# VectorE's order in eight recurrence units: masks, states, subtractions, then the next unit's products and scans

## The chip, the cores and the metric

The kernel runs on one core of one Trainium2 chip. The metric is device time in microseconds (us), the median of several runs. Five engines work side by side and each runs its own instructions strictly in the order in which they were written out: TensorE (PE, matrix products), VectorE (DVE), ScalarE (ACT), GpSimd (POOL), and SyncE (SP), which here only issues DMA transfers. They wait for one another through semaphores.

## The reference

The inputs pass through three layers. The first is a recurrence over 768 tokens (2 sequences, 8 heads of width 48) with a state of 48 by 48 per head; the second a gated two-layer product (weights `w_k`, `w_r`, `w_v`); the third a gated layer with mixing over tokens (`w_in`, `w_sg`, `w_out`).

```python
for t in range(S):                                   # layer 1
    cur = einsum('bhd,bhe->bhde', u * k_t, v_t)
    y[:, :, t] = einsum('bhd,bhde->bhe', r_t, state + cur)
    state = w_t[..., None] * state + einsum('bhd,bhe->bhde', k_t, v_t)
# layer 2, x_prev = x shifted by one token
xk = mu_k * x + (1 - mu_k) * x_prev
xr = mu_r * x + (1 - mu_r) * x_prev
x = sigmoid(xr @ w_r) * (relu(xk @ w_k) ** 2 @ w_v)
# layer 3
u, v = split(gelu(x @ w_in));  v = layernorm(v) * g
out = x + (u * (w_sg @ v + b_sg)) @ w_out
```

## The kernel before

**Units of the recurrence.** The tokens are cut into four groups of 384, and the eight heads into four pairs. A unit is one pair of heads in one group; the code numbers units from 0 to 15, four to a group, and so does this text (the units 9 to 16 of the change's description, counted from one, are the code's 8 to 15). A unit treats its 384 tokens as three chunks of 128 and replaces the loop over t by scans and matrix products:

- *Scans* on VectorE (`scans`, L444 to L449): running products of the decay, forward (`pf`) and backward (`pr`), with a small reciprocal between them.
- *Products* (`products`, L453 and L456): `kp` = k times `pr`, `rp` = r times `pf`.
- Step S on TensorE (`attn_sc`): it transposes `kp` (`kt_ps`, L476), forms the bonus `ab` from two halves of r times k times u (`rh`; the high half by ScalarE at L521, the low one by VectorE at L523; L495 and L496 read them), and multiplies `kp` with `rp` (`sc`, L500).
- *Masks* on VectorE (L532): `am`, the causal part of `sc`. Just ahead of them VectorE multiplies `ab` with v (L503, tile `ru`). GpSimd's only piece of a unit is the product `ru` of the next unit (L466); it may start when L503 is done, and the halves `rh` of the next unit follow it.
- Step K (`attn_kv`): state increments `kv` (L552). *States* on VectorE (L562 and L564): `zt`, the state after each chunk; ScalarE scales them into `sblk` and `scar` (L578), four and two small copies per unit.
- Step Y (`attn_y`): v times `am` (L596). Step Z (`attn_z`): the scaled states times `rp` are added (L610). VectorE then adds the bonus (`yo`, L620), and SyncE copies `yo` to its place in `xx` (L631).

**The projections beside them.** Layer 2 of group s runs on TensorE between the steps of the four units of group s+1. In the stretch of this study these are products of 128 by 128 by 384 in pieces: every weight and every activation is held as a high and a low half (a value rounded to a shorter format and what is left), and each product is three matrix products. The pieces: eight blocks `k`, three blocks `r`, three blocks `v`. After each `k` block ScalarE does three operations (`kr` relu, L735; `kh` square into the high half, L756; `kr` square in place, L757), and VectorE the *subtraction* `kl` = square minus high half (L758). Two buffers hold `kr`, so the relu of block f waits for the subtraction of block f-2. The low halves of the weights (`wkl`, `wrl`, `wvl`, one subtraction each at L332) are made once, in the units 8 to 11: 8 + 3 + 8 of them.

**What sets the order.** TensorE's instructions are written by hand in the order of `plan`. For the other engines the code gives each instruction a due time (`at`), and a list scheduler writes each engine's order from due times and dependencies; `tc.issue_after(x)` forbids the scheduler to place an instruction ahead of x on its engine, without a wait. In the main loop (from L1040 on) the names `kd` and `g` are the step and the unit after which a piece is called: `prep` is scans and products at once, and `UPIN` is the unit from which on they are called apart. Loads go one unit ahead into rings of three buffers (`uw`, `urk`); a load waits until the buffer's last reader is done. `top` (L325) and `wf` (L327) on ScalarE and VectorE unpack weights that a DMA has brought into `stg`, those of layer 3 (`w_in`) among them.

Of the kernel before, what the change touches and what calls it, by code (L numbers as in the profile page):

```python
# [6 lines left out]
F32 = mybir.dt.float32  # L7
F32R = mybir.dt.float32r
# [6 lines left out]
ALU = mybir.AluOpType  # L15
# [29 lines left out]
B_AM = 2  # L45
B_KP = 3
T_START = 7
UPIN = 11
T_GAP = 2.5
T_TAIL = 9.0  # L50
VQ = 4
# [19 lines left out]
def emit(tc, tin, nin, vt, consts, ucp, pars, b_sg, w_k, w_v, w_r, w_in, w_sgT, w_out, outT):  # L71
# [263 lines left out]
    def full1(nm, i, shape):  # L335
        wt[nm, i] = (pl["w"].tile(shape, F32, name="w" + nm, tag="wl", bufs=NW1 + SPARE),)

    def split_rv(s):
        with tc.issue_after(st[s * NP]["am"]), tc.issue_after(head["khi"]):
            for f in range(KM):  # L340
                split1("r", f, TS["r", s, f], V)
            for f in range(NVN // 2):
                split1("v", f, TS["v", s, 0] + f * 0.49, V)

    def split_v(s):
        with tc.issue_after(st[s * NP + 1]["am"]):
            for f in range(NVN // 2, NVN):
                split1("v", f, TS["v", s, 0] + f * 0.49, V)

    def split1(nm, i, dl, e=PL):  # L350
        if not split_ops[0]:
            return
        full = wt[nm, i][0]
        shape = list(full.shape)
        lo = pl["w"].tile(shape, F32R, name="w" + nm + "l", tag="wl", bufs=NW1 + SPARE)
        if early["hi"] % 2 == 0:
            early["t"] = pair()
        o = early["hi"] % 2 * WT
        early["hi"] += 1
        hi = early["t"][:, o:o + WT].rearrange("p (c f) -> p c f", c=shape[1])  # L360
        ins = split_to(hi, lo, full, dl, e)
        wt[nm, i] = (hi, lo)
        return ins

    def conv_moe1(first=0, last=2 * KF + KM):
# [375 lines left out]
    def moe1_sq(s, f, kr):  # L741
        nt = subs[s][2] * CH
        te, tv = TE["k", s, f], TS["v", s, 0] + f * MM[s, "v"]
        vn = is_nat(s, "v") and (f < NVN or not split_ops[0])
        kh = pl["w"].tile([128, nt], F32 if vn else F32R, name="kh", tag="kh", bufs=KF)
        dl = min(te + 1, tv - 2)
        if vn:
            with at(dl):
                A.activation(kh, kr, AF.Square)
            m1[s, "k", f] = (kh,)  # L750
            return
        if f % 2 == 0:
            m1[s, "kl"] = klpair(F32R)
        kl = m1[s, "kl"][:, f % 2 * WT:f % 2 * WT + nt]
        with at(dl):
            A.activation(kh, kr, AF.Square)  # L756
            A.activation(kr, kr, AF.Square)  # L757
            V.tensor_tensor(kl, kr, kh.bitcast(F32), ALU.subtract)  # L758
        m1[s, "k", f] = (kh, kl)

    def moe1_r(s, j, c=None):
        nt = subs[s][2] * CH
# [8 lines left out]
    def moe1_v(s, j, q):  # L771
        g, c0, n = subs[s]
        js = slice(j * 128, (j + 1) * 128)
        if q == 0:
            m1[s, "ps"] = mm_tile()[:, 0:n * CH]
        ps = m1[s, "ps"]
        fs = range(q * KF // VQ, (q + 1) * KF // VQ)
        mm(ps, [(part(wt["v", f], slice(None), 0, js), m1[s, "k", f]) for f in fs], q == 0, q == VQ - 1)
        if q < VQ - 1:
            return  # L780
        with at(TE["v", s, j] - 0.5):
            V.tensor_tensor(x2[g][:, j, c0 * CH:(c0 + n) * CH], ps, m1[s, "r", j], ALU.mult)
        if s == NAT["r"] - 1 and j == KM - 1 and split_ops[0]:
            with tc.issue_after(st[2 * NP - 1]["ev"]), tc.issue_after(st[2 * NP - 1]["sa"]):
                for f in range(KF):
                    head["khi"] = split1("k", f, TS["k", s + 1, f], V)

    m2 = {}

# [231 lines left out]
    def products(i):  # L1021
        for _ in head["prep", i]:
            pass
# [26 lines left out]
    for n, key in enumerate(keys[:n_in]):  # L1050
# [45 lines left out]
        if kd == "S" and g == NP:  # L1096
            prep(NP + 1)
            conv_moe1(3)
        if kd == "S" and g >= UPIN - 1 and g + 1 < NU:
            with tc.issue_after(st[g]["am"]):  # L1100
                products(g + 1)
        if kd == "K" and g == 2 * NP:
            split_rv(g // NP)
        if kd == "K" and g == 2 * NP + 1:
            split_v(g // NP)
        if kd == "Z" and g == 2 * NP - 2:
            scans(2 * NP)
        elif kd == "Z" and g == 2 * NP - 1:
            with tc.issue_after(st[g]["ev"]):
                products(2 * NP)  # L1110
                prep(2 * NP + 1)
        elif kd == "Z" and g >= NP and g + 2 < UPIN:
            prep(g + 2)
        elif kd == "Z" and g >= NP and g + 2 < NU:
            with tc.issue_after(st[g]["zt"]):
                scans(g + 2)
        if kd == "Z" and g >= NP:
            if g % NP == NP - 1:
# [8 lines left out]
                        mk[2]()  # L1127
                    mr[2]()
                else:
                    moe1_prep(g // NP, 0, [()] + 2 * [(st[g]["zt"], st[g]["sa"])])  # L1130
        if kd == "S":
            head["unit"] = g
            if "sq" in head:
                with behind():
                    head.pop("sq")()
        if kd == "K":
            head["unit"] = None
        if kd == "k" and key[2:] in ((0 if g in (0, NS - 1) else KM - 1,), (0 if g in (0, NS - 1) else KM - 1, KM - 1)) and g != 1:
            moe1_prep(g, 1, [] if g in (0, NS - 1) else [(m1[g, "ev", f],) for f in range(KM)])
        if kd == "v" and g == NS - 2 and key[2:] == (KM - 1, VQ - 1):  # L1140
# [87 lines left out]
```

## Time and profile before

| What | Value |
|---|---|
| median of 3 runs | 342.83 us (342.09 to 343.37) |
| the profiled execution, its own time | 341.94 us |
| its span in the trace | 340.2 us |
| TensorE busy | 327.9 us, 96% |
| VectorE busy | 240.4 us, 71% |
| ScalarE busy | 189.0 us, 56% |
| mean granted TensorE clock | 0.995 |

The span is the time that the trace covers; the execution's own time is 1.74 us longer. Busy shares are means over stages of quite different kinds: from 200 us on TensorE runs without a pause, while between 80 and 171 us it pauses now and then for a unit's masks or states. In the trace an instruction that waited carries in brackets the idle time before it and who released it.

### The profile page before, as it was taken

The numbers are of one execution on the slowest core, as the hardware profiler recorded it, in microseconds if no ns is written. First come the engines' busy times: TensorE is split into PE (matmuls) and PEld (weight loads), VectorE is DVE, ScalarE is ACT, GpSimd is POOL, SyncE is SP. The second block draws the span as 40 slices with busy tenths as digits, with TensorE's granted clock in tenths as the row PEclk, the third lists the DMA queues.
The fourth block names the chain that finished last, engine by engine and source line by source line (L and its number), as shares of the span: only waits on it lengthen the run. The fifth ranks groups of instructions, "written<-read, shape, count | busy, mean of one in ns | idle before, by whom it ended". The sixth has DMA issues, their size and how long they took to land.

```text
span 340.2 us, 5953 instructions
## 1 busy us (share of the span) xinstructions
PE 327.9 (96%) x2139; PEld 286.5 (84%) x2139; DVE 240.4 (71%) x537; ACT 189.0 (56%) x447; POOL 38.3 (11%) x60
## 2 busy tenths in 40 slices
PE   7999999999999899999999999999999999999993
PEld 3785666666878799987899999989999999999993
DVE  5988989779989973988349552698889833645531
ACT  3567985669577753977438983867443216211100
POOL 3210203010211100121013431000000000000000
PEclk9999999999999999999999999999999999999997
DMA  8779864756222460011014414613230010100022
GB/s 213 207 245 307 282 195 107 196 139 181 87 75 78 107 180 19 17 36 37 19 66 141 138 46 134 187 41 82 61 81 22 1 69 2 46 25 0 0 74 77
DMA packets 23878, 34.22 MB, mean 101 GB/s; under 512 B 3440, under 2 KB 18160, under 8 KB 23840
## 3 DMA queue, kind: packets, MB, share of 16 engines
q1 hardware_dynamic: 21696, 31.34, 31.2%
q10 hardware_dynamic: 2144, 2.41, 2.8%
q8 instruction: 19, 0.31, 0.4%
q14 instruction: 19, 0.16, 0.2%
HBM read 29.02 MB, written 2.36 MB: 92 GB/s over the span
## 4 chain that ended last, share of the span: by engine, by line
PE 61%; issue 12%; DVE 11%; ACT 6%; DMA 5%; POOL 2%; SPq 1%; ACTq 0%; POOLq 0%; DVEq 0%
PE mm L657 30%; PE mn L657 28%; DVE pf L444 2%; ACT top L325 2%; DMA urk<-tin 2%; DVE am L532 2%; POOL ru L466 2%; DVE pr L449 1%; DMA uv<-nin 1%; DMA xx<-yo 1%; PE sc L500 1%; ACT sblk L578 1%; DMA uw<-tin 1%; PE y L596 1%; DVE kl L758 1%
## 5 line engine op out<-in xcount | busy, mean ns | idle before, releaser
L645 ACT ACTIVATE gah<-gt 128x384 fp32r<-128x384 f32 x16 | 8.4, 526 | 43.7 <-DVE gt L853 43.7
L466 POOL TENSOR_TENSOR ru<-urk 112x384 f32<-112x384 f32 x15 | 18.8, 1256 | 111.5 <-DVE ru L503 81.0
L578 ACT ACTIVATE sblk<-zt,pf 48x48 f32<-48x48 f32 x62 | 20.4, 329 | 10.0 <-DVE zt L562 5.3
L657 PE MATMUL mm<-kh,wh 128*128 128x384 f32 x64 | 22.0, 343 | 0.0
L657 PE MATMUL mm<-kh,wvl 128*128 128x384 f32 x64 | 21.6, 337 | 0.0
L657 PE MATMUL mm<-kl,wh 128*128 128x384 f32 x64 | 21.5, 337 | 0.0
L758 DVE TENSOR_TENSOR kl<-kr,kh 128x384 fp32r<-128x384 f32 x24 | 14.5, 606 | 8.6 <-ACT kr L757 8.5
L657 PE MATMUL mm<-xkh,wh 128*128 128x384 f32 x57 | 20.5, 360 | 0.0
L657 PE MATMUL mn<-wsh,vl 128*128 128x384 f32 x60 | 20.0, 334 | 0.0
L657 PE MATMUL mn<-wsh,vh 128*128 128x384 f32 x60 | 20.0, 334 | 0.0
L657 PE MATMUL mn<-wsl,vh 128*128 128x384 f32 x60 | 20.0, 334 | 0.0
L657 PE MATMUL mm<-xkh,wkl 128*128 128x384 f32 x57 | 19.2, 337 | 0.0
L657 PE MATMUL mm<-xkl,wh 128*128 128x384 f32 x57 | 19.2, 336 | 0.0
L444 DVE TENSOR_TENSOR_SCAN pf<-uw,d1f 112x387 f32<-112x387 f32 x16 | 15.9, 991 | 2.5 <-DMA uw<-tin 2.5
L532 DVE TENSOR_TENSOR am<-sc,cst 128x384 f32<-128x384 f32 x32 | 16.2, 546 | 1.3 <-PE sc L500 1.3
L332 POOL TENSOR_TENSOR w2l<-wf,w2h 128x384 fp32r<-128x384 f32 x12 | 12.9, 1088 | 37.0 <-ACT w2h L331 37.0
L657 PE MATMUL mm<-xkh,wk 128*128 128x384 f32 x48 | 17.0, 497 | 0.0
L657 PE MATMUL mm<-kh,wv 128*128 128x384 f32 x48 | 16.3, 490 | 0.0
L693 DVE SCALAR_TENSOR_TENSOR dx<-xx,par,dx 128x384 f32<-128x384 f32 x18 | 10.7, 610 | 7.2 <-ACT dx L691 7.2
L691 ACT ACTIVATE dx<-xx,par 128x384 f32<-128x384 f32 x22 | 12.9, 608 | 4.9 <-DMA xx<-yo 4.8
L610 PE MATMUL y<-rp,sblk 112*112 112x128 f32 x64 | 12.0, 293 | 3.7 <-ACT sblk L578 2.4
L449 DVE TENSOR_TENSOR_SCAN pr<-uw,d1r 112x387 f32<-112x387 f32 x16 | 15.3, 959 | 0.3
(223 smaller groups left out, 981.8 us busy)
## 6 DMA issues: line engine op xcount, KB each, us to landing
urk<-tin SPq DMA_DIRECT2D x26, 144.0 KB, 3.0
wh<-w_k SPq DMA_DIRECT2D x8, 384.0 KB, 5.4
stg<-w_in SPq DMA_DIRECT2D x8, 384.0 KB, 4.5
wq<-tin SPq DMA_DIRECT2D x16, 168.0 KB, 2.4
wsf<-w_sgT SPq DMA_DIRECT2D x12, 192.0 KB, 4.1
outT<-ot SPq DMA_DIRECT2D x12, 192.0 KB, 1.9
uv<-nin ACTq DMA_DIRECT2D x14, 144.0 KB, 3.7
uw<-tin SPq DMA_DIRECT2D x26, 72.8 KB, 2.6
```

The costliest lines, as they stand in the source:

```text
L332: e.tensor_tensor(lo, full, hi.bitcast(F32), ALU.subtract)
L444: V.tensor_tensor_scan(pf[:, 0:n1], w[:, 0:n1], d1f[:, 0:n1], 1.0, ALU.mult, ALU.max)
L449: V.tensor_tensor_scan(pr[:, 1:wl][:, ::-1], w[:, 1:wl][:, ::-1], dr[:, 1:wl][:, ::-1], 0.0, ALU.mult, ALU.add)
L466: return e.tensor_tensor(rks[i], urk[i][:, 0], urk[i][:, 1], ALU.mult).ins
L532: s["am"] = V.tensor_tensor(am[:, h], sc[h], mask, ALU.mult).ins
L578: s["sa"] = A.activation(sb[hs, hs], o[hs], AF.Copy, scale=s["pe"][c][hs]).ins
L610: PE.matmul(y3[0:PR, c], s["us"][c], s["rp"][:, c], start=False, stop=(c == cs[-1]), skip_group_check=True)
L645: A.activation(hi, src, AF.Copy)
L657: PE.matmul(ps, l, r, start=(first and k == 0), stop=(last and k == len(prods) - 1))
L691: ins = [A.activation(d, xj[:, 1 + t0:1 + t1], AF.Copy, scale=mu[:, j:j + 1]).ins]
L693: V.scalar_tensor_tensor(ops[0][:, j] if nat else d, xj[:, t0:t1], nu[:, j:j + 1], d, ALU.mult, ALU.add)
L758: V.tensor_tensor(kl, kr, kh.bitcast(F32), ALU.subtract)
```

## The change

The order of the pieces on VectorE, ScalarE and SyncE is changed for the units 8 to 15; TensorE's and GpSimd's orders stay word for word the same, and no arithmetic is added or removed.

- The `kl` subtractions that fall inside a unit's S to K stretch are collected and placed behind the unit's states (`issue_after(st[g]["zt"])`).
- In the units 8 to 10 and 12 to 14 the next unit's products are placed behind the states; the scans of the unit after it follow at Z (`scans(g + 2)`). `prep`, which called both at once and early, is kept only up to unit 9. At the change of groups (after unit 11) the order is scans of 12, products of 12, scans of 13.
- The weights' high halves are still all made at once, but the low halves are collected in `lows` and given out: five `wkl` at once (`LO_HEAD`), three subtractions behind the states of unit 8, three of unit 9, four of unit 10, the last four behind the masks of unit 11 (`LO_AT`, `LO_LAST`).
- The first of the three `xk` preparations of the next group is tied to the states of unit g-1.

```diff
-UPIN = 11
+LO_AT = {8: 3, 9: 3, 10: 4}
+LO_LAST = 11
+LO_HEAD = 5
...
+    lows = []
+
+    def split_rv():
+        with tc.issue_after(head["khi"]):
+            for nm, n in (("r", KM), ("v", NVN)):
+                for f in range(n):
+                    split1(nm, f, TS[nm, 1, f if nm == "r" else 0], V, True)
+
+    def split_lo(n, behind_):
+        with tc.issue_after(behind_):
+            for f in lows[:n]:
+                f()
+        del lows[:n]
...
+        if later:
+            lows.append(low)
+        else:
+            low()
...
             A.activation(kh, kr, AF.Square)
             A.activation(kr, kr, AF.Square)
-            V.tensor_tensor(kl, kr, kh.bitcast(F32), ALU.subtract)
+
+        def low():
+            with at(dl):
+                V.tensor_tensor(kl, kr, kh.bitcast(F32), ALU.subtract)
+
         m1[s, "k", f] = (kh, kl)
+        if split_ops[0] and s and (head.get("unit") or 0) > NP and (s, f) not in hold_sq:
+            head.setdefault("kl", []).append(low)
+        else:
+            low()
...
-                    head["khi"] = split1("k", f, TS["k", s + 1, f], V)
+                    head["khi"] = split1("k", f, TS["k", s + 1, f], V, f >= LO_HEAD)
...
-        if kd == "S" and g >= UPIN - 1 and g + 1 < NU:
-            with tc.issue_after(st[g]["am"]):
+        if kd == "K" and 2 * NP <= g and g + 1 < NU and g != 3 * NP - 1:
+            with tc.issue_after(st[g]["zt"]):
                 products(g + 1)
         if kd == "K" and g == 2 * NP:
-            split_rv(g // NP)
-        if kd == "K" and g == 2 * NP + 1:
-            split_v(g // NP)
+            split_rv()
+        if kd == "K" and g in LO_AT:
+            split_lo(LO_AT[g], st[g]["zt"])
...
                 products(2 * NP)
-                prep(2 * NP + 1)
-        elif kd == "Z" and g >= NP and g + 2 < UPIN:
+                scans(2 * NP + 1)
+        elif kd == "Z" and g == 3 * NP - 1:
+            with tc.issue_after(st[g]["zt"]):
+                scans(g + 1)
+                products(g + 1)
+                scans(g + 2)
+        elif kd == "Z" and g == 3 * NP - 2:
+            pass
+        elif kd == "Z" and NP <= g < 2 * NP:
             prep(g + 2)
...
-                    moe1_prep(g // NP, 0, [()] + 2 * [(st[g]["zt"], st[g]["sa"])])
+                    moe1_prep(g // NP, 0, [(st[g - 1]["zt"], st[g - 1]["sa"])] + 2 * [(st[g]["zt"], st[g]["sa"])])
         if kd == "S":
             head["unit"] = g
+            if g == LO_LAST:
+                split_lo(NVN, st[g]["am"])
...
         if kd == "K":
             head["unit"] = None
+            for f in head.pop("kl", []):
+                with tc.issue_after(st[g]["zt"]):
+                    f()
```

VectorE in unit 8, from the scan of unit 10 (before) and from unit 8's bonus product (after) on; `am` are unit 8's masks, `zt` and `zcar` its states, `kl` the subtractions of blocks 0 to 2, `kp` and `rp` unit 9's products in the changed order (unit 10's in the order before). Before:

```order
150 L449 SCALAR_TENSOR_TENSOR pr<-uw_106,d1r 112x387
151 L332 TENSOR_TENSOR wkl<-wk,wh 128x384
152 L532 TENSOR_TENSOR am<-sc,cst 128x384 x2
153 L758 TENSOR_TENSOR kl<-kr,kh 128x384
154 L523 SCALAR_TENSOR_TENSOR rh<-ru,cst,rh 112x384
155 L758 TENSOR_TENSOR kl<-kr,kh 128x384
156 L562 COPY zt<-kv 112x48
157 L453 TENSOR_TENSOR kp<-urk_109,pr 112x384
158 L564 SCALAR_TENSOR_TENSOR zt<-zt,pf,kv 112x48
159 L332 TENSOR_TENSOR wrl<-wr,wh 128x384
160 L758 TENSOR_TENSOR kl<-kr,kh 128x384
161 L564 SCALAR_TENSOR_TENSOR zcar<-zt,pf,kv 112x48
```

The same place after the change:

```order
142 L517 TENSOR_TENSOR ru<-ab,uvt 112x384
143 L546 TENSOR_TENSOR am<-sc,cst 128x384 x2
144 L775 TENSOR_TENSOR kl<-kr,kh 128x384
145 L576 COPY zt<-kv 112x48
146 L578 SCALAR_TENSOR_TENSOR zt<-zt,pf,kv 112x48
147 L578 SCALAR_TENSOR_TENSOR zcar<-zt,pf,kv 112x48
148 L775 TENSOR_TENSOR kl<-kr,kh 128x384
149 L467 TENSOR_TENSOR kp<-urk_108,pr 112x384
150 L470 TENSOR_TENSOR rp<-urk_108,pf 112x384
151 L775 TENSOR_TENSOR kl<-kr,kh 128x384
152 L537 SCALAR_TENSOR_TENSOR rh<-ru,cst,rh 112x384
153 L368 TENSOR_TENSOR wkl<-wk,wh 128x384
```

The scan and the weight subtraction ahead of the masks are gone, the three states stand together with one subtraction ahead of them instead of two, and the low half `rh` of the next unit has moved from behind the first subtraction to behind the third.

ScalarE in unit 9: relu, square and square in place of blocks 4 and 5, the four `sblk` and the `scar` copies. Before:

```order
147 L735 ACTIVATE kr<-mm 128x384
148 L756 ACTIVATE kh<-kr 128x384
149 L757 ACTIVATE kr<-kr 128x384
150 L735 ACTIVATE kr<-mm 128x384
151 L756 ACTIVATE kh<-kr 128x384
152 L757 ACTIVATE kr<-kr 128x384
153 L578 ACTIVATE sblk_88<-zt,pf 48x48 x2
154 L578 ACTIVATE sblk_89<-zt,pf 48x48 x2
155 L274 DMA uv<-nin 128x288
156 L578 ACTIVATE scar_83<-zcar,pf 48x48
```

The same place after the change:

```order
148 L749 ACTIVATE kr<-mm 128x384
149 L770 ACTIVATE kh<-kr 128x384
150 L771 ACTIVATE kr<-kr 128x384
151 L749 ACTIVATE kr<-mm 128x384
152 L770 ACTIVATE kh<-kr 128x384
153 L592 ACTIVATE sblk_88<-zt,pf 48x48 x2
154 L592 ACTIVATE sblk_89<-zt,pf 48x48 x2
155 L771 ACTIVATE kr<-kr 128x384
156 L592 ACTIVATE scar_83<-zcar,pf 48x48 x2
```

The square in place of block 5, which its `kl` subtraction reads, has moved behind the four `sblk` copies.

ScalarE at the change of groups, behind unit 11: `dx` and `xkh` prepare the next group's `xk` (three pieces), `top` unpacks `w_in`, `kr` is the relu of the next group's block 0. Before:

```order
184 L325 ACTIVATE top_129<-stg 128x384
185 L696 ACTIVATE xkh<-dx 128x384
186 L325 ACTIVATE top_128<-stg 128x384
187 L691 ACTIVATE dx<-xx_79,par 128x384
188 L696 ACTIVATE xkh<-dx 128x384
189 L735 ACTIVATE kr<-mm 128x384
190 L691 ACTIVATE dx<-xx_79,par 128x384
```

The same place after the change:

```order
183 L710 ACTIVATE xkh<-dx 128x384
184 L327 ACTIVATE top_129<-stg 128x384
185 L705 ACTIVATE dx<-xx_79,par 128x384
186 L710 ACTIVATE xkh<-dx 128x384
187 L327 ACTIVATE top_128<-stg 128x384
188 L749 ACTIVATE kr<-mm 128x384
189 L705 ACTIVATE dx<-xx_79,par 128x384
```

The second `top` stood two instructions ahead of the last `xk` piece and now stands behind it, directly ahead of the relu of block 0.

## Rows read from the trace of the kernel before

**Rows 1.** The page, part 1: busy us, share of span, instructions

```profile
PE 327.9 (96%) x2139; PEld 286.5 (84%) x2139; DVE 240.4 (71%) x537; ACT 189.0 (56%) x447; POOL 38.3 (11%) x60
```

**Rows 2.** Windows: stretch, length, busy of PE, PEld, DVE, ACT, POOL, clock, DMA

```profile
80.00:100.00 20.00, 19.29 (x127) 15.40 (x126) 18.71 (x41) 15.58 (x38) 2.42 (x2) 1.00 0.40 117
100.00:120.00 20.00, 18.53 (x152) 15.89 (x151) 18.94 (x42) 14.03 (x35) 2.97 (x3) 1.00 0.36 94
200.00:330.00 130.00, 130.00 (x715) 125.40 (x714) 80.57 (x214) 49.95 (x114) 6.98 (x16) 1.00 0.19 56
```

**Rows 3.** Timeline of PE: start, us, instruction; starts of step S, units 8 to 15

```profile
87.01 0.45 PE L476 MATMUL kt_ps<-cst,kp 112*128 112x112 f32 x3
...
96.96 0.45 PE L476 MATMUL kt_ps<-cst,kp 112*128 112x112 f32 x3
...
106.20 0.45 PE L476 MATMUL kt_ps<-cst,kp 112*128 112x112 f32 x3
...
115.32 0.45 PE L476 MATMUL kt_ps<-cst,kp 112*128 112x112 f32 x3
...
135.07 0.45 PE L476 MATMUL kt_ps<-cst,kp 112*128 112x112 f32 x3
...
143.38 0.45 PE L476 MATMUL kt_ps<-cst,kp 112*128 112x112 f32 x3
...
152.82 0.45 PE L476 MATMUL kt_ps<-cst,kp 112*128 112x112 f32 x3
...
162.03 0.45 PE L476 MATMUL kt_ps<-cst,kp 112*128 112x112 f32 x3
```

**Rows 4.** Timeline of PE: steps Y and Z that waited

```profile
91.50 1.32 PE L596 MATMUL y<-am,uv 128*64 128x128 f32 x12
...
96.65 0.47 PE L610 MATMUL y<-rp,sblk 112*112 112x128 f32 x2 [0.64 <-ACT sblk L578]
...
161.73 0.47 PE L610 MATMUL y<-rp,sblk 112*112 112x128 f32 x2 [0.64 <-DVE xkl L697]
```

**Rows 5.** Timeline of DVE in unit 8

```profile
89.57 0.95 DVE L449 TENSOR_TENSOR_SCAN pr<-uw,d1r 112x387 f32<-112x387 f32 x1
90.44 0.53 DVE L332 TENSOR_TENSOR wkl<-wk,wh 128x384 fp32r<-128x384 f32 x1
90.89 1.01 DVE L532 TENSOR_TENSOR am<-sc,cst 128x384 f32<-128x384 f32 x2
91.82 0.55 DVE L758 TENSOR_TENSOR kl<-kr,kh 128x384 fp32r<-128x384 f32 x1
92.52 0.62 DVE L523 SCALAR_TENSOR_TENSOR rh<-ru,cst,rh 112x384 fp32r<-112x384 f32 x1
94.01 0.56 DVE L758 TENSOR_TENSOR kl<-kr,kh 128x384 fp32r<-128x384 f32 x1 [0.87 <-ACT kr L757]
94.48 0.20 DVE L562 COPY zt<-kv 112x48 f32<-112x48 f32 x1
```

**Rows 6.** Timeline of ACT in unit 8

```profile
92.39 0.47 ACT L735 ACTIVATE kr<-mm 128x384 f32<-128x384 f32 x1
92.89 0.53 ACT L756 ACTIVATE kh<-kr 128x384 fp32r<-128x384 f32 x1
93.45 0.53 ACT L757 ACTIVATE kr<-kr 128x384 f32<-128x384 f32 x1
...
94.82 0.66 ACT L578 ACTIVATE sblk<-zt,pf 48x48 f32<-48x48 f32 x2
```

**Rows 7.** Timeline of POOL: the product ru in units 8, 9 and 10

```profile
89.73 2.10 POOL L466 TENSOR_TENSOR ru<-urk 112x384 f32<-112x384 f32 x1 [19.33 <-DVE ru L503]
99.68 1.26 POOL L466 TENSOR_TENSOR ru<-urk 112x384 f32<-112x384 f32 x1 [7.85 <-DVE ru L503]
109.53 1.01 POOL L466 TENSOR_TENSOR ru<-urk 112x384 f32<-112x384 f32 x1 [8.59 <-DVE ru L503]
```

**Rows 8.** DMA issues, 60 to 180 us: count, KB each, median us to landing

```profile
stg<-w_in SPq DMA_DIRECT2D x6, 384.0 KB, 5.1
```

More of the change, by code (lines that the diff above doesn't have):

```diff
@@ L336, in full1, with split1 @@
         wt[nm, i] = (pl["w"].tile(shape, F32, name="w" + nm, tag="wl", bufs=NW1 + SPARE),)
[L338 to L350, printed above, removed]
+    lows = []
[9 more added lines that the diff above has]
+        del lows[:n]
+    def split1(nm, i, dl, e=PL, later=False):
         if not split_ops[0]:
@@ L354, in split1 @@
         shape = list(full.shape)
-        lo = pl["w"].tile(shape, F32R, name="w" + nm + "l", tag="wl", bufs=NW1 + SPARE)
         if early["hi"] % 2 == 0:
@@ L360, in split1 @@
         hi = early["t"][:, o:o + WT].rearrange("p (c f) -> p c f", c=shape[1])
-        ins = split_to(hi, lo, full, dl, e)
-        wt[nm, i] = (hi, lo)
+        def low():
+            lo = pl["w"].tile(shape, F32R, name="w" + nm + "l", tag="wl", bufs=NW1 + SPARE)
+            with at(dl):
+                e.tensor_tensor(lo, full, hi.bitcast(F32), ALU.subtract)
+            wt[nm, i] = (hi, lo)
+        with at(dl):
+            ins = A.activation(hi, full, AF.Copy).ins
+        if later:
+            lows.append(low)
+        else:
+            low()
         return ins
@@ L757, in moe1_sq, with low @@
             A.activation(kr, kr, AF.Square)
-            V.tensor_tensor(kl, kr, kh.bitcast(F32), ALU.subtract)
+        def low():
+            with at(dl):
+                V.tensor_tensor(kl, kr, kh.bitcast(F32), ALU.subtract)
         m1[s, "k", f] = (kh, kl)
+        if split_ops[0] and s and (head.get("unit") or 0) > NP and (s, f) not in hold_sq:
+            head.setdefault("kl", []).append(low)
+        else:
+            low()
     def moe1_r(s, j, c=None):
```

## The prediction

> **What bounds the kernel now.** I read the page's busy shares first, then the windows by stage, then TensorE's timeline in the stage that has pauses, and last the other engines' timelines around those pauses. TensorE is busy for 96% of the span [rows 1], and from 200 us on it has no pause at all: 130.00 us with 715 matrix products, 0.18 us each, at a granted clock of 1.00 [rows 2]. The change touches nothing there. Between 80 and 120 us TensorE idles for 0.71 and 1.47 us of two stretches of 20, while VectorE is busy for 18.71 and 18.94 of 20 [rows 2]: here VectorE decides when TensorE's next step may start.
>
> How much TensorE loses there is read best from the starts of step S [rows 3], since a busy row hides part of a wait. Unit 12 runs undisturbed: 135.07 to 143.38, so 8.31 us. Units 8, 9 and 13 hold the same products and take 9.95, 9.24 and 9.44; units 10 and 14 hold three products fewer (0.55 less, so 7.76) and take 9.12 and 9.21. The losses are 1.64, 0.93, 1.13, 1.36 and 1.45, together 6.5 us. That is the most the change can give: at the execution's own 341.94 it would leave 335.4. Units 11, 12 and 15 lose nothing.
>
> The waits are of two kinds [rows 4]: in unit 8 step Y takes 1.32 us because its masks are late, and step Z waits for scaled states (0.64 in unit 8; the one at 161.73 is put down to a VectorE subtraction, behind which ScalarE's state copies stood). VectorE's timeline shows why [rows 5]: unit 8's masks, whose step S began at 87.01, start only at 90.89, behind a scan and a weight subtraction; the states start at 94.48, behind a subtraction that waited 0.87 for ScalarE's square.
>
> **The change part by part.** No engine gets more or less work, and TensorE's order is the same, so only waits change. VectorE's steps, start to start [rows 5]: scan 0.87, subtraction or product 0.45 to 0.47, masks 0.93, low half `rh` 0.53 to 0.62; three states some 0.7 (estimate, from 0.20 for one and the wait of each for the last). ScalarE [rows 6]: relu 0.50, square 0.56, square in place 0.53, so 1.6 a block; four state copies 1.3.
>
> *Unit 8, gain 1.64.* Nothing but the bonus product stands before the masks now; they run at about 88.7 to 89.7, step Y wants them at 91.2. The states follow the increments at 91.5, the copies run 92.5 to 93.8, step Z is due at 94.8. Both waits go; unit 9's step S starts at 95.3 instead of 96.96.
>
> *What is late next: `rh`.* The low half of the next unit's bonus now stands behind the third subtraction, and on ScalarE that block's last square stands behind the four copies. In unit 8: GpSimd's product ends at 89.5, ScalarE's `rh` at 90.1, block 1 at 91.7, relu and square of block 2 at 92.5, copies at 93.85, last square at 94.4, subtraction 94.9, `rh` 95.5. TensorE reads it behind `kt_ps` (0.45 [rows 3]), about half a us after S starts, at 95.75: it just fits. In unit 9 VectorE does `rh`, a weight subtraction, a scan and `yo` before the bonus product (from 94.9: 0.53 + 0.45 + 0.87 + 0.47, so it starts at 97.3 and ends at 97.8). Then GpSimd 1.26 [rows 7], ScalarE's `rh` to 99.7, block 4 to 101.2 (its relu overlaps), relu and square of block 5 to 102.1, copies to 103.45, square 104.0, subtraction 104.5, `rh` 105.1. Step S of unit 10 starts at 103.8 (0.2 late, for the last copy) and wants `rh` at 104.2: a new wait of 0.9 to 1.0. Nothing in the trace of before shows this wait. Its bounds are nothing, if the square runs ahead of the copies' end, and 1.8, if GpSimd needs 2.10 instead of 1.26 [rows 7]; I take 1.0, by the row whose product also ran beside one subtraction and the masks (1.26). In unit 10 the products stand behind that last subtraction as well, but its block ends early; what is left is 0.35 for the copies, behind a sigmoid on ScalarE, and 0.1 for `rh` in unit 11.
>
> What GpSimd's product costs hangs on VectorE: 2.10 us at 89.73, beside a scan and a subtraction [rows 5, 7], and 1.01 at 109.53. The Trainium skill, "GPSIMD Engine Reference", Specifications, says that GpSimd shares its interfaces to the on-chip memory with VectorE and is held up by VectorE instructions with two inputs there; the trace agrees. By it the sum would stay at 1.26 in units 9 and 10 (one such subtraction stands beside the product) and fall to 1.01 in unit 8; a version that put more subtractions there would pay 0.84 more per unit.
>
> *Weights' halves.* The fourteen that are moved (three `wkl`, three `wrl`, eight `wvl`) come 1 us and more ahead of their first product by the same walk (the last `wkl` ends at 101.5, TensorE wants it at 102.4): cost nothing, hidden by TensorE's blocks ahead of them. If one came late, its block would wait at most the 0.47 of a subtraction or two.
>
> *Scans and products.* VectorE's 37.65 us of work in 80 to 120 [rows 2] would not fit into the some 36 that this stretch shrinks to, but unit 12's scans and products (two of 0.87, two of 0.47 and a reciprocal, 2.8 us) move behind unit 11, where TensorE has only `v` and `k` blocks until unit 12's step S. Loads: each scan's buffer is filled a unit or more ahead, so they stay hidden; the copy of unit 11's `yo` now goes out ahead of the `w_in` load instead of behind it.
>
> *The change of groups.* Unit 13's scan now stands ahead of the unpacking `wf`, which by the walk starts at about 126.7. The `w_in` load, which waits for that buffer, goes out at 127.2 and lands 5.1 later [rows 8], at 132.4. ScalarE's second `top` waits for it, and in the new order the relu of the next block 0 and a piece `dx` stand behind it: 133.0, 133.5, 134.0. VectorE idles until then, so unit 12's bonus product comes 1.9 us after its step S (132.7). VectorE has no slack after that: unit 12's masks are just in time, unit 13's end at 146.4 where step Y wants them at 145.1 (wait 1.3, and 0.25 more for copies), unit 14's are 0.8 late and its copies 0.55. Below, this costs nothing if the load lands before ScalarE gets there; above, every us that it lands later costs one.
>
> *Sum.* Waits gone: 6.5. Waits in their place: 0.2 + 1.0 (unit 9 to 10), 0.35 + 0.1 (10 to 11), 1.3 + 0.25 (13), 0.8 + 0.55 (14), together 4.55. Gain 1.95. On the execution's own 341.94 that is 340.0; the median of the runs shown, 342.83, lies 0.89 above that execution, so the forecast for a median is 340.9.
>
> **The rivals.**
>
> *A. The load is no obstacle.* ScalarE's `top` finds `w_in` landed, or VectorE makes up the delay. Then unit 13 and 14 keep only their copies' waits and a little of the masks: 1.3 + 0.6 of the 4.55 go, gain 3.9, median 338.9. For it: 5.1 is a median under heavy traffic. Against it: two instructions moved in front of the buffer's release.
>
> *B. Given back.* The `rh` wait appears in units 8, 9 and 10, about 1.0 us each, instead of once: 2.0 more, gain nothing, 342.8. For it: in unit 8 the slack is only 0.2 us, and GpSimd at 2.10 instead of 1.01 eats it four times over (the rule named above is this rival's mechanism). Against it: beside the masks GpSimd took 1.01.
>
> *C. Slower.* The third subtraction decides in every unit of both groups. At 1.8 us each (GpSimd at 2.10) in the six units 8 to 10 and 12 to 14 these waits make 10.8 in place of the 1.1 that I count; with the other 3.45 that is 14.2, less 6.5: 7.7 slower. At 1.0 each it is 6.0 + 3.45 - 6.5, so 3.0 slower, median 345.8, which I take. It decides from 0.8 us in each of the six units on. Against it: in units 12 to 14 there are gaps on ScalarE ahead of the copies, and where TensorE waits, the next unit's chain gets that time back.
>
> That the change doesn't do what it says is excluded: its rows show the states and masks moved, on the engines that TensorE waits for.
>
> **How the numbers follow.** Forecast 0.50, A 0.20, B 0.20, C 0.10. The forecast's own range is 339.7 to 342.0 (each of the three big terms may be off by 0.5 or so). The range over all cases is 338.6 to 343.6: it reaches past A and B and leaves out the far ends of A and C. 0.5% is 1.7 us, about what a measurement of this kernel can tell from no change: faster by more needs a median under 341.1. Two thirds of the forecast's chance lie there (0.33) and all of A (0.20): 0.53. Within 0.5%: the rest of the forecast and B, 0.37. Slower: C, 0.10.
>
> **What would show it.** In the trace of after the starts of step S give each unit's length: unit 8 should fall to about 8.3 and unit 9 to about 8.5, unit 10 hold a wait of `ab` for VectorE's `rh` of about 1 us, and unit 13's step Y a wait for the masks of about 1.3. ScalarE's `top` should wait for `stg` just before that, and the relu of block 0 behind it start near 133. TensorE's time from 171 us on should be shifted as a whole, not changed. I am wrong if the units 8 to 10 still take over 9 us each, if `ab` waits in more than one unit, or if a weight's low half or a load shows as what TensorE waits for.

## The result and the profile after

The changed kernel takes 338.77 us (median of 4 runs, 338.41 to 339.43), the kernel before on the same chip 342.46 (4 runs, 341.57 to 343.37): a ratio of 0.9894 with a 95% interval of 0.9862 to 0.9927, so 3.7 us faster. The forecast was 340.9; the measured time lies below the forecast's own range (339.7 to 342.0), inside the range over all cases (338.6 to 343.6), and next to rival A's 338.9. The profiled execution of the changed kernel took 338.41 us, its span is 336.6.

Page part 1 of the changed kernel answers to [rows 1]: the numbers of instructions are the same, in a span 3.6 us shorter; GpSimd alone is busy for clearly less, 36.4 us instead of 38.3.

```profile
PE 326.6 (97%) x2139; PEld 286.6 (85%) x2139; DVE 239.7 (71%) x537; ACT 189.1 (56%) x447; POOL 36.4 (11%) x60
```

Its windows by stage answer to [rows 2] (columns as there). TensorE idles for nothing in the first stretch and for 1.16 us in the second, against 0.71 and 1.47. From 200 us on TensorE has no pause, as before.

```profile
80.00:100.00 20.00, 20.00 (x154) 16.73 (x153) 16.63 (x35) 16.99 (x42) 2.35 (x2) 1.00 0.43 126
100.00:120.00 20.00, 18.84 (x155) 16.60 (x155) 18.82 (x45) 13.44 (x35) 2.35 (x2) 1.00 0.36 92
200.00:330.00 130.00, 130.00 (x715) 125.39 (x714) 79.84 (x212) 47.35 (x109) 4.58 (x14) 1.00 0.19 56
```

TensorE's starts of step S, units 8 to 15, answer to [rows 3]. Their differences are the first two lines of the table in the next section.

```profile
86.52 0.45 PE L490 MATMUL kt_ps<-cst,kp 112*128 112x112 f32 x3
...
94.72 0.45 PE L490 MATMUL kt_ps<-cst,kp 112*128 112x112 f32 x3
...
103.41 0.45 PE L490 MATMUL kt_ps<-cst,kp 112*128 112x112 f32 x3
...
112.53 0.45 PE L490 MATMUL kt_ps<-cst,kp 112*128 112x112 f32 x3
...
132.34 0.45 PE L490 MATMUL kt_ps<-cst,kp 112*128 112x112 f32 x3
...
140.65 0.45 PE L490 MATMUL kt_ps<-cst,kp 112*128 112x112 f32 x3
...
149.47 0.45 PE L490 MATMUL kt_ps<-cst,kp 112*128 112x112 f32 x3
...
158.48 0.45 PE L490 MATMUL kt_ps<-cst,kp 112*128 112x112 f32 x3
```

From unit 8 to unit 15 TensorE needs 71.96 us instead of 75.02: 3.06 gained. The last start stands 3.55 earlier; the other 0.49 lies before unit 8. On VectorE and ScalarE the order differs from some 80 us on, but unit 8's start lies between 86.45 and 87.06 in all thirteen profiles of this study, and a kernel with the change in it has the latest (`uv` by SyncE, 87.06). So these 0.49 are taken for scatter between executions and not for a gain of the change.

VectorE in unit 8 answers to [rows 5]. The masks start 1.70 us after step S instead of 3.88, the states 4.50 instead of 7.47; the third subtraction waits 0.71 for ScalarE, and `rh` stands behind it, as forecast.

```profile
88.22 1.02 DVE L546 TENSOR_TENSOR am<-sc,cst 128x384 f32<-128x384 f32 x2 [0.30 <-PE sc L514]
...
91.02 0.21 DVE L576 COPY zt<-kv 112x48 f32<-112x48 f32 x1 [1.31 <-PE kv L566]
...
93.95 0.56 DVE L775 TENSOR_TENSOR kl<-kr,kh 128x384 fp32r<-128x384 f32 x1 [0.71 <-ACT kr L771]
94.43 0.61 DVE L537 SCALAR_TENSOR_TENSOR rh<-ru,cst,rh 112x384 fp32r<-112x384 f32 x1
```

TensorE around the end of unit 9 answers to [rows 4]. Step Z waits 0.23 for the copies of the states, and the wait of `ab` for `rh` that the prediction had put there stands in the third line.

```profile
102.49 0.39 PE L624 MATMUL y<-rp,sblk 112*112 112x128 f32 x2
103.11 0.47 PE L624 MATMUL y<-rp,sblk 112*112 112x128 f32 x2 [0.23 <-ACT sblk L592]
...
104.78 0.43 PE L510 MATMUL ab<-rh,hblk 112*112 112x384 f32 x1 [0.74 <-DVE rh L537]
```

Over the whole kernel step Z's waits for the copies (us, times, longest) fall from 2.4 in six places to 0.8 in four. The first row is of the kernel before, the second of the changed one.

```profile
PE y L610 <- ACT sblk L578: 2.4, 6, 0.6
PE y L624 <- ACT sblk L592: 0.8, 4, 0.2
```

At the change of groups SyncE issues the `w_in` load at 126.88, and ScalarE unpacks it at 129.84 with no wait in front of it: 2.96 us after its issue (the DMA view gives 2.9 to landing), where the prediction had taken 5.1 [rows 8]. The relu behind it waits for TensorE's product and not for the load. The first row is SyncE's, the other two are ScalarE's.

```profile
126.88 0.88 SPq L316 DMA_DIRECT2D stg<-w_in  x2
```

```profile
129.84 0.65 ACT L327 ACTIVATE top<-stg 128x384 f16<-128x384 bf16 x1
131.49 0.49 ACT L749 ACTIVATE kr<-mm 128x384 f32<-128x384 f32 x1 [1.00 <-PE mm L671]
```

In the kernel before, the same load took 5.3 us, and ScalarE waited for it:

```profile
123.07 0.88 SPq L314 DMA_DIRECT2D stg<-w_in  x2
```

```profile
128.38 0.65 ACT L325 ACTIVATE top<-stg 128x384 f16<-128x384 bf16 x1 [3.32 <-DMA stg<-w_in]
```

Unit 13's masks in the changed kernel run just ahead of step Y, which shows no wait for them (the first row is VectorE's, the second TensorE's):

```profile
143.81 1.01 DVE L546 TENSOR_TENSOR am<-sc,cst 128x384 f32<-128x384 f32 x2
```

```profile
144.79 0.94 PE L610 MATMUL y<-am,uv 128*64 128x128 f32 x12
```

### The profile page after: what moved, and what is told of

Same layout as the page of the kernel before. It is cut to its first block, busy times and chain, and to the rows that moved or that the text cites. A ratio compares the mean times of both kernels' runs of the same rounds, so it can differ in the third digit from the quotient of the medians.

```text
span 336.6 us, 5952 instructions
## 1 busy us (share of the span) xinstructions
PE 326.6 (97%) x2139; PEld 286.6 (85%) x2139; DVE 239.7 (71%) x537; ACT 189.1 (56%) x447; POOL 36.4 (11%) x60
## 4 chain that ended last, share of the span: by engine, by line
PE 65%; DVE 11%; issue 11%; DMA 5%; ACT 4%; POOL 2%; SPq 1%; POOLq 0%; ACTq 0%; DVEq 0%
PE mn L671 28%; PE mm L671 27%; DMA stg<-w_v 2%; DVE pf L458 2%; POOL ru L480 2%; PE y L624 2%; PE sc L514 2%; PE y L610 2%; DMA cst<-consts 2%; PE y L613 1%; DVE kl L775 1%; DVE pr L463 1%; DVE am L546 1%; DVE wvl L368 1%; PE mm L690 1%
## 5 line engine op out<-in xcount | busy, mean ns | idle before, releaser
L480 POOL TENSOR_TENSOR ru<-urk 112x384 f32<-112x384 f32 x15 | 16.9, 1125 | 113.1 <-DVE ru L517 66.0
L514 PE MATMUL sc<-rp,kp 48*128 48x128 f32 x192 | 15.0, 289 | 0.0
```

What stands on the lines that cost most here:

```text
L480: return e.tensor_tensor(rks[i], urk[i][:, 0], urk[i][:, 1], ALU.mult).ins
L514: PE.matmul(sc[h][:, c], s["kp"][hs, c], s["rp"][hs, c], start=True, stop=True)
```

## The experiments

The table has the length of each unit in us (difference of the starts of step S in the profile; unit 11 holds the change of groups), the median, and the ratio to the kernel before on the same chip with its 95% interval. TensorE's order is the same in all of them. The medians come from several chips, on which the kernel before took 341.83 to 342.50: medians less than some 0.7 apart are not told apart by themselves. The unit lengths come from one profiled execution each.

| Kernel | 8 | 9 | 10 | 11 | 12 | 13 | 14 | median | ratio |
|---|---|---|---|---|---|---|---|---|---|
| before | 9.95 | 9.24 | 9.12 | 19.75 | 8.31 | 9.44 | 9.21 | 342.46 | 1 |
| after | 8.20 | 8.69 | 9.12 | 19.81 | 8.31 | 8.82 | 9.01 | 338.77 | 0.9894 (0.9862 to 0.9927) |
| late load | 8.20 | 8.68 | 9.12 | 19.81 | 8.31 | 9.13 | 9.01 | 338.93 | 0.9898 (0.9879 to 0.9918) |
| `rh` first | 8.19 | 8.20 | 8.53 | 19.81 | 8.31 | 8.82 | 8.99 | 337.62 | 0.9861 (0.9840 to 0.9882) |
| subtractions as before | 8.20 | 8.64 | 9.53 | 19.75 | 8.31 | 9.14 | 9.55 | 339.78 | 0.9926 (0.9907 to 0.9945) |
| halves not rationed | 8.19 | 9.24 | 8.52 | 20.29 | 8.31 | 8.82 | 9.01 | 338.98 | 0.9912 (0.9894 to 0.9929) |
| scans as before | 8.51 | 8.21 | 8.59 | 19.75 | 8.31 | 9.48 | 7.90 | 337.71 | 0.9882 (0.9858 to 0.9906) |
| subtractions alone | 10.17 | 8.62 | 7.81 | 19.76 | 8.31 | 9.48 | 8.67 | 339.48 | 0.9933 (0.9919 to 0.9946) |
| halves alone | 9.28 | 8.20 | 8.82 | 20.04 | 8.31 | 9.45 | 8.44 | 338.94 | 0.9912 (0.9896 to 0.9927) |
| scans alone | 8.72 | 9.31 | 8.61 | 20.29 | 8.31 | 9.12 | 9.78 | 340.59 | 0.9961 (0.9946 to 0.9976) |
| `rh` and `pr` | 8.19 | 8.21 | 8.53 | 19.82 | 8.30 | 8.83 | 8.54 | 337.50 | 0.9854 (0.9833 to 0.9876) |
| `uv` by SyncE | 8.19 | 8.20 | 8.52 | 19.82 | 8.31 | 8.83 | 8.53 | 337.54 | 0.9863 (0.9843 to 0.9884) |
| high `rh` later | 8.19 | 8.20 | 7.81 | 20.22 | 8.31 | 8.42 | 7.77 | 335.57 | 0.9818 (0.9802 to 0.9834) |

**Late load.** Is the time at which `w_in` lands what the forecast's missing 2 us hang on? SyncE issues the load twice, so that the tile is complete only with the second transfer.

```diff
-        with at(ld):
-            SP.dma_start(stg.bitcast(U16)[:, 1:1 + 4 * WT], src.bitcast(U16))
+        for _ in range(2 if split_ops[0] and n_ == NW1 + 3 else 1):
+            with at(ld):
+                SP.dma_start(stg.bitcast(U16)[:, 1:1 + 4 * WT], src.bitcast(U16))
```

> The fourth w_in load of the change of groups, which lands at 129.84 us in the changed kernel (2.96 us after its issue), is issued a second time into the same tile behind the first, so that it lands about 3 us later, near the 132.4 us that the prediction took. Nothing else is moved. Theory (the forecast's missing time is this load's landing): ScalarE's second `top` copy then ends near 133.5, its square and `dx` come behind that, the masks of unit 13 come late, and unit 13 (8.82 us now) takes 0.8 to 1.3 us more, so the kernel takes 339.5 to 340.2 us, 0.7 to 1.4 more than the changed kernel's 338.8. Rival (the landing is no obstacle whatever its time, because ScalarE has the slack to catch up): unit 13 stays within 0.2 us of 8.82 and the kernel at 338.6 to 339.0 us.

ScalarE's timeline of this kernel shows the late landing as a wait. But the relu and `dx` now stand ahead of the late unpacking.

```profile
131.92 0.49 ACT L750 ACTIVATE kr<-mm 128x384 f32<-128x384 f32 x1 [1.75 <-PE mm L672]
132.31 0.61 ACT L706 ACTIVATE dx<-xx,par 128x384 f32<-128x384 f32 x1
133.55 0.65 ACT L328 ACTIVATE top<-stg 128x384 f16<-128x384 bf16 x1 [0.64 <-DMA stg<-w_in]
```

Unit 13 takes 0.31 more, because its masks come that much later against step Y, and the median is 0.16 higher, which the intervals don't tell apart. The theory's 0.7 us or more did not come. The order was not held as intended: the program's scheduler moved the relu ahead of the late unpacking, so the case that the prediction feared (a late load with the relu behind it) was not run. What is shown: a landing some 3.3 us later, with the relu ahead of it, costs 0.3 us in unit 13, and unit 14 takes 9.01 us either way.

**`rh` first.** The low half `rh` of the next unit goes ahead of the third subtraction in units 8 and 9 (the instruction is remembered as `lo`, and the third subtraction issued behind it).

```diff
+            if "kl3" in head:
+                with tc.issue_after(st[g]["lo"]):
+                    head.pop("kl3")()
...
-            for f in head.pop("kl", []):
+            kls = head.pop("kl", [])
+            if len(kls) == 2:
+                head["kl3"] = kls.pop()
+            for f in kls:
...
```

> On VectorE the low half `rh` of the next unit goes ahead of the third `kl` subtraction in units 8 and 9; TensorE's order is untouched. Theory (the third subtraction waits for ScalarE's square behind the four state copies, and `rh` stands behind it): the wait of `ab` for `rh` after unit 9 goes, 0.74 us in the profile, unit 10 begins 0.7 to 1.0 us earlier, and since the stages up to 162 us pass the shift on, the kernel takes 337.8 to 338.1 us. Rival (the state copies of unit 9 on ScalarE end late anyway and TensorE meets another wait at once): unit 10's first `kt_ps` moves by less than 0.3 us or unit 10 takes as much longer, and the kernel stays at 338.5 to 339.0 us.

TensorE's timeline of this kernel, the same place as above:

```profile
102.84 0.60 PE L624 MATMUL y<-rp,sblk 112*112 112x128 f32 x4
...
103.74 0.34 PE L510 MATMUL ab<-rh,hblk 112*112 112x384 f32 x1
```

The wait of `ab` is gone, unit 10 is 0.59 us shorter and unit 9 0.49 as well; the median is 1.15 lower than the changed kernel's and just below the theory's 337.8 to 338.1. So the third subtraction cost 1.08 us, half of it where no row names it: its wait of 0.71 in unit 8 pushed everything that VectorE did next, masks and states of unit 9 included, and so the copies that TensorE waited for at 103.11.

**One part undone.** Three kernels, each with one part of the change taken back. Subtractions:

```diff
-        if split_ops[0] and s and (head.get("unit") or 0) > NP and (s, f) not in hold_sq:
-            head.setdefault("kl", []).append(low)
-        else:
-            low()
+        low()
```

> Undoes one part alone: the `kl` subtractions of units 8 to 14 are no longer held until behind the unit's states; weights' rationing and the early masks stay. Theory (each subtraction placed ahead of `zt` holds the states while it waits for ScalarE's square): `zt` comes later by one subtraction with its wait, 0.3 to 0.7 us, in about four units, partly covered by 0.7 us less at the `rh` wait after unit 9; the kernel takes 339.2 to 340.5 us. Rival (the masks are all that counts and a subtraction ahead of the states finds its square done): no loss, and the `rh` wait gone besides: 337.8 to 338.5 us.

Rationing:

```diff
-LO_AT = {8: 3, 9: 3, 10: 4}
+LO_AT = {8: 14}
```

> Undoes one part alone: the 14 low halves of weights (0.55 us each, 7.7 us of VectorE) are no longer rationed over four units but all allowed from behind unit 8's states on, so that the scheduler puts them wherever VectorE looks free; masks, subtractions and scans stay as in the changed kernel. Theory (what matters is that masks and states stand ahead, and a low half ahead of a state pushes it by 0.47): units 9 to 11 lose up to 0.5 us each where a low half has slid ahead of a state, in sum 0.3 to 1.2 us; the kernel takes 339.1 to 340.0 us. Rival (VectorE has room behind the states in every unit, and the rationing does nothing): 338.6 to 338.9 us, within 0.1 of the changed kernel.

Scans and products (the conditions at Z and S again as before):

```diff
-        if kd == "K" and 2 * NP <= g and g + 1 < NU and g != 3 * NP - 1:
-            with tc.issue_after(st[g]["zt"]):
+        if kd == "S" and g >= 10 and g + 1 < NU:
+            with tc.issue_after(st[g]["am"]):
                 products(g + 1)
...
```

> Undoes one part alone: the scans and products of the coming units stand where they stood before the change, ahead of the masks of the running unit; the subtractions stay behind the states and the weights rationed. Theory (the scans and products ahead of the masks are what made TensorE's third product wait before): unit 8 takes 1.4 to 1.8 us more than its 8.20 us, units 13 and 14 0.5 to 1.2 us more together, and the kernel takes 340.8 to 342.0 us, most of the way back to 342.3. Rival (the subtractions held behind the states are the larger part, and scans ahead of the masks fit in VectorE's idle time): units 8, 13 and 14 within 0.4 us of the changed kernel's, 338.8 to 339.6 us.

The subtractions behaved as the theory had it: 339.78, and TensorE's waits for the copies grow from 0.8 to 1.2 us. The rationing lies between the two expectations: 0.2 us over the changed kernel, with unit 9 0.55 longer, unit 10 0.60 shorter and unit 11 0.48 longer, so the halves only shift the waits. The scans overturned the theory: with scans and products back in front the kernel takes 337.71, below even the rival's range and 1.06 less than the changed kernel. The two ratios' intervals overlap; the profiles agree with the medians, as units 8 to 14 take 70.75 us together instead of 71.96. VectorE in unit 8 of that kernel shows why:

```profile
87.90 0.95 DVE L463 TENSOR_TENSOR_SCAN pr<-uw,d1r 112x387 f32<-112x387 f32 x1
88.78 0.53 DVE L517 TENSOR_TENSOR ru<-ab,uvt 112x384 f32<-112x384 f32 x1
89.22 1.01 DVE L546 TENSOR_TENSOR am<-sc,cst 128x384 f32<-128x384 f32 x2
90.15 0.66 DVE L775 TENSOR_TENSOR kl<-kr,kh 128x384 fp32r<-128x384 f32 x1
91.08 0.62 DVE L537 SCALAR_TENSOR_TENSOR rh<-ru,cst,rh 112x384 fp32r<-112x384 f32 x1 [0.27 <-ACT rh L535]
91.62 0.55 DVE L467 TENSOR_TENSOR kp<-urk,pr 112x384 f32<-112x384 f32 x1
92.09 0.20 DVE L576 COPY zt<-kv 112x48 f32<-112x48 f32 x1
```

The masks start 2.63 us after step S, 0.9 later than in the changed kernel, and the unit is only 0.31 longer: that much earlier than step Y they need not be. In return `rh` runs at 91.08 and 99.06, ahead of the third subtraction, and units 9 and 10 pay nothing for it. The kernel with `rh` first keeps scans and products behind the states, has `rh` ahead as well, and takes 337.62: the same. So what the third part cost is the place of `rh` that came with it; with that mended, what it gains in units 8 and 13 (0.98) and loses in unit 14 (1.09) about cancels.

**One part alone.** The kernel before with one part each: subtractions held behind the states, halves rationed (with the `xk` preparation tied as in the change), scans and products behind the states.

> The kernel before with one part of the change alone: the `kl` subtractions of units 8 to 14 held until behind the unit's states; weights' halves, scans and products stand as before. Theory (formed on the run with early scans: that run kept this part and the rationing and gained 4.8 us, so the gain lies in these two, and most of it in the states no longer waiting behind subtractions): the waits of TensorE's last products for ScalarE's copies of the states, 2.4 us in six places, fall to under 1 us; the kernel gains 1.5 to 2.5 us on before's 342.4, 339.9 to 340.9. Rival (the weights' halves that stand ahead of masks and states are the larger part): this alone gains under 0.8 us, 341.6 to 342.4.

> One part of the change alone: the low halves of weights behind the states and rationed over units 8 to 11 (and the first mixed input of the group that begins in unit 12 held as in the change); subtractions, scans and products stand as before. Theory (the subtractions ahead of the states are the larger part): this alone gains 1.0 to 2.0 us on before's 342.4, 340.4 to 341.4, and unit 8, where four low halves stood ahead of the masks, goes from 9.95 to under 9 us. Rival (the halves are the larger part): 338.5 to 340 us. With the run of subtractions alone it shows whether the two parts add up to the 4.8 us of the run with both.

> The kernel before with the third part of the change alone: the coming units' scans and products behind the running unit's states; subtractions and weights' halves stand as before. Theory (by the run with early scans this part costs 1.1 us once the other two are in, and each of the other two alone gains 2.4 to 2.9; the three parts do not add up): where it stands alone the masks of unit 8 come about 1.5 us earlier and that unit gains 0.7 to 1.3 us, while the next unit's `kp` and `rp`, `rh` now wait behind subtractions that wait for ScalarE, and units 9, 10 and 13 lose as much or more: 341.3 to 343 us against before's 342. Rival (early masks are worth as much as the other parts when alone): 339.3 to 340.5 us.

Against before on the same chip the subtractions alone gain 2.40 us, the halves alone 2.94, the scans alone 1.24. The first two nearly add up (5.3, and 4.8 in the run that has both); with the scans the sum would be 6.6, and the change has 3.7. For the halves the rival held (338.5 to 340), the scans lie between their two expectations. The waits of TensorE in the kernel with the subtractions alone (engine, waiting and awaited, us, times, longest):

```profile
PE y L610 <- ACT sblk L578: 0.8, 2, 0.6
PE y L610 <- DVE xkl L697: 0.6, 1, 0.6
PE y L610 <- DVE kl L761: 0.6, 1, 0.6
```

The copies cost 0.8 in two places where before had 2.4 in six; the two waits put down to VectorE are there before too. Unit 8 keeps its loss (10.17), because there the place of the subtractions is taken by halves:

```profile
93.52 0.20 DVE L562 COPY zt<-kv 112x48 f32<-112x48 f32 x1
93.64 0.55 DVE L332 TENSOR_TENSOR wrl<-wr,wh 128x384 fp32r<-128x384 f32 x1
94.10 0.26 DVE L564 SCALAR_TENSOR_TENSOR zt<-zt,pf,kv 112x48 f32<-112x48 f32 x1
```

**Towards a better order.** Three kernels on top of `rh` first; the second and the third contain the first. In the first, the backward scan `pr` of unit 15 goes behind unit 14's states:

```diff
-        next(head["prep", i])
+        if i - 1 not in (14,):
+            next(head["prep", i])
```

> The `rh` order of the run before the last (low half ahead of the third `kl`) and, besides, the backward scan `pr` of unit 15 moved behind unit 14's states on VectorE, so that unit 14's masks come about 0.9 us earlier. Theory: besides the 0.7 to 1.0 us at unit 10, unit 14 (9.01 us) loses its late `y` (about 0.45 us) and some of the two waits for ScalarE's state copies (about 0.6 us): unit 14 at 8.0 to 8.5 us and the kernel at 337.0 to 337.6 us. Rival (the scan moved behind the states delays unit 15's products, and what unit 14 gains unit 15 gives back): unit 14 shorter but the last step at 162 us no earlier than by unit 10's part: 337.8 to 338.1 us.

Unit 14 is 0.45 shorter, with a new wait of 0.36 for `kp` at its end; the median is only 0.12 below that of `rh` first, less than the runs can tell apart. In the second, SyncE issues `uv`:

```diff
-        e = SP if i < 2 else A
+        e = SP if i < 2 or i >= 3 * NP - 1 else A
```

> The version with `rh` and `pr` moved, and besides the loads of `uv` for units 11 to 15 issued by SyncE in place of ScalarE, where each issue stands for 0.33 us among the four state copies of a unit. Theory (the last state copy of unit 10 is late by that issue, and TensorE's last products wait 0.23 us and restart): the wait in unit 10 goes, unit 10 at 8.1 to 8.4 us in place of 8.53, and the kernel takes 337.0 to 337.3 us. Rival (the copies are late by what stands ahead of them on ScalarE, the evictions, and not by the issue; or the loads now stand behind others in SyncE's queue and come late): unit 10 within 0.1 us of 8.53 or a new wait for `uv`, 337.4 to 338 us.

The rival held: unit 10 is 8.52 and keeps its wait of 0.23. Unit 10's four copies take 1.36 us without the issue among them and, in the first of the three kernels, 1.37 with it (109.89 to 111.26): the issue in ScalarE's queue did not hold ScalarE up. What is left is what stands ahead of the copies, and there ScalarE had waited 1.69 us for GpSimd's `ru`; the next kernel tests it. The third kernel moves the high half `rh` behind a block that is ready before:

```diff
-        with at(TS["S", i] - 2):
+        with at(TS["S", i] - 2), tc.issue_after(head["sqs"][-1 if i % 4 == 3 else -2]) if split_ops[0] and i > 2 * NP and i % 4 else contextlib.nullcontext():
             A.activation(hi, rks[i], AF.Copy, scale=u)
...
-            A.activation(kr, kr, AF.Square)
+            head.setdefault("sqs", []).append(A.activation(kr, kr, AF.Square).ins)
```

> The version with `rh`'s low half and `pr` moved, and besides, on ScalarE, the high half `rh` of the next unit, which waits for GpSimd's `ru` (ScalarE idle 1.7 us in front of it in units 9 and 10, 2.0 us in unit 14), behind a block of ReLU and squares that is ready before. Theory (what makes the four state copies late is the ScalarE work that queues behind this wait): the copies end 0.5 to 1 us earlier in units 9 to 14, the waits of 0.16 to 0.23 us and their restarts in units 10 and 13 go, units 10, 13 and 14 together 0.6 to 1.4 us shorter, and the kernel takes 336.2 to 337.0 us. Rival (units 10, 13 and 14 are long for another reason, the masks): they stay within 0.2 us and the kernel at 337.3 to 337.7 us.

ScalarE in unit 10 of that kernel: the block of relu and squares runs while GpSimd works, `rh` follows without a wait, and now the copies wait for the state instead of the state for the copies.

```profile
105.47 0.49 ACT L749 ACTIVATE kr<-mm 128x384 f32<-128x384 f32 x1
106.00 0.53 ACT L770 ACTIVATE kh<-kr 128x384 fp32r<-128x384 f32 x1
106.55 0.53 ACT L771 ACTIVATE kr<-kr 128x384 f32<-128x384 f32 x1
107.14 0.62 ACT L535 ACTIVATE rh<-ru,cst 112x384 fp32r<-112x384 f32 x1
107.67 0.47 ACT L790 ACTIVATE rs<-mm 128x384 f32<-128x384 f32 x1
109.11 1.04 ACT L592 ACTIVATE sblk<-zt,pf 48x48 f32<-48x48 f32 x3 [0.97 <-DVE zt L576]
```

It takes 335.57 us, below the expected range: 6.3 us less than before on its chip. TensorE's waits, whole kernel:

```profile
PE mm L1027 <- DVE mm L1067: 1.8, 1, 1.8
PE ab L510 <- DVE rh L537: 0.2, 1, 0.2
```

Its units 8 to 10 and 12 to 14 take 48.70 us together. That is the undisturbed length which the prediction had worked out (four times 8.31 and twice 7.76, 48.76), so the measure by which it counted losses was sound.

## Why the forecast came out 2 us high

- **What bounds the kernel, and 6.5 us at most.** Held: the kernel with the late high `rh` gets all of it in these units (55.27 to 48.70), and its median is 6.3 us lower.
- **Unit 8, gain 1.64.** Held (8.20, nothing lost). The runs show how much each part does: the unit takes 9.28 with the halves moved alone, 8.72 with the scans, 10.17 with the subtractions, 8.51 with halves and subtractions, 8.20 with halves and scans. So what stood ahead of the masks counted, and the second subtraction ahead of the states costs nothing once halves and scans are gone.
- **What is late next: `rh`.** Held in mechanism and place, and in the sum (1.2 forecast, 1.08 measured), not in its parts: forecast 0.2 in unit 9 and 1.0 at `ab`, and the run that takes it away gains 0.49 and 0.59. GpSimd's product, on which it hung, took 1.02 us in unit 8 and 1.32 and 1.33 in units 9 and 10, where 1.01 and 1.26 were taken; rival B needed 2.10 in unit 8. It was not given back in units 8 to 10 alike (rival B) nor in six units (rival C): `ab` waits once.
- **The rest of unit 10, forecast 0.35 and 0.1.** Too small: without the `rh` wait the unit still loses 0.77 (8.53 against 7.76). That unit 10 as a whole loses 1.36 where 1.35 was forecast is luck: the `ab` wait was 0.4 smaller, the rest 0.4 larger. The run with the high `rh` later shows what was missed: the idle 1.7 us of ScalarE in front of that instruction, behind which the evictions and then the copies queued.
- **Weights' halves at no cost.** Held: TensorE waits for none of them in the changed kernel.
- **Scans and products fit.** They do, since unit 11's length is unchanged. That moving them is no gain once the other two parts are in, but costs about 1 us (338.77 against 337.71) through the place of `rh`, the forecast did not see, as it counted by units and not by parts.
- **The change of groups: the step that failed.** The forecast let `w_in` land 5.1 us after its issue, the median of six such loads, and charged 1.3 for unit 13's masks, 0.8 for unit 14's. It landed 2.9 us after its issue, before ScalarE came to it, and unit 12's bonus product came 0.84 us after its step S and not 1.9. Unit 13's masks start at 143.81 and end about when step Y begins (144.79), and the unit loses 0.51 instead of 1.55. This is the term that was mis-sized.
- **Unit 14: the right size for a wrong reason.** It loses 1.25, where 1.35 was forecast as a consequence of the late load. The load was not late, and a load 3.3 us later changed nothing here (9.01). Moving the scan `pr` of unit 15 takes 0.45 off, moving the high `rh` on ScalarE the rest (7.77): the loss came from what stood ahead of unit 14's masks and copies.
- **The sum.** Waits left from unit 8 to 15: forecast 4.55, measured 3.45 (-0.11 in unit 8, 0.38, 1.36, 0.06 in unit 11, 0.51 and 1.25). The gain there is 3.06 in place of 1.95, and 1.04 of the difference of 1.1 is unit 13. The forecast's median is 2.1 too high: 1.1 is this, 0.37 is the kernel before, whose median is now 342.46 and not 342.83, and the rest lies in no unit; the stretch before unit 8 alone scatters by 0.6 from one profile to the next.
- **Rival A.** Its condition came true (`top` found `w_in` landed), and its 338.9 was met in part by luck: it had units 13 and 14 lose 1.0 together, they lose 1.76, and its gain of 3.9 stands against 3.06 in the units.

What stays open: what a landing at 132.4 would cost with ScalarE's relu behind it, as the late-load run did not make that order; and why the load landed sooner than in the kernel before, for which only the traffic is on record (last section).

## What to carry to other kernels

Where an engine with a fixed order waits for another (here VectorE's third subtraction, ScalarE's high `rh`), what counts is less the wait itself than what is queued behind it and who waits for that; put work that is ready in front of it. Take parts of a reordering back one at a time: two of the three here were worth 4.8 us together, and the third, put on top of them, gave about 1 of it back. When a transfer decides, give its time a range and look at what else moves at that moment in the new order: here a median of six such loads, and the same load in the kernel before (5.3), both missed.

## What the runs showed that was not expected

- A short wait of TensorE costs more than its row says. In the changed kernel step Z of unit 9 shows a wait of 0.23, but from 102.49 to the next step S at 103.41 it takes 0.92, against 0.43 without it (102.84 to 103.27 in `rh` first): 0.49. The wait of 0.18 for `rh` in the last kernel goes with a unit 11 that is 0.41 longer.
- One and the same load of 384 KB took 5.3 us to land before and 2.9 after the change. From its issue to its landing the DMA engines moved 245 GB/s over 5.31 us before and 220 GB/s over 2.92 us after, so 1.3 and 0.64 MB (estimate from these two): before, more other data moved beside it.
- GpSimd's seven products `ru`, one in each of the units 8 to 14, took 1.00 to 1.33 us in the changed kernel, where before one took 2.10 [rows 7] and one 1.73.
